# Alternating the second stage's half products with the next pair's gated tiles

## The chip, the cores and the metric

The kernel runs on one core of one Trainium2 chip. The metric is the device time of one execution in microseconds (us). The kernel before took 1480.34 us (median of 3 runs, 1479.32 to 1481.01).

## The reference, cut to what matters

Three blocks follow one another: an attention over 32 memory slots, a gated feed-forward block (512 to 1536 to 512) and a second feed-forward block (512 to 2048 to 512). The change is in the middle block.

```
a = softmax(phi);  k_m = a^T k;  v_m = a^T v            # 8 batches, 8 heads, 576 rows, 32 slots
attn = softmax(q k_m^T / 8);  x = attn v_m              # x: 4608 tokens x 512
g = x @ w_gate;  val = x @ w_val                        # 512 x 1536 each
y = (silu(g) * val) @ w_out                             # 1536 x 512   <- the change is here
h = y @ w_in;  out = elu(h) @ w_out2                    # 512 x 2048, 2048 x 512
```

## The kernel before, in words

All matrix products are made of float32 parts: every operand is split into a high part (`hh`, `hi`) and a low part (`hl`, `lo`), and three matmuls stand for one. The kernel has three stages.

**Stage one** (to about 328 us) does the attention for the 8 batches and the first 4 of the 12 units (128 columns of the hidden dimension) of the gated block, with their share of the output product, which is stored in `p1_d` in DRAM. At its end begins the conversion of weights: a "set" (`sets`, L210) fetches 1 MB of 64-bit weights into a raw tile `wr`, puts float32 numbers into the tile `uq` (`words`, L116, four VectorE instructions; L139 one more), forms eight combinations (`set_split`, L190) and splits them into four tiles `uw`, which the ScalarE queue stores to DRAM (`store_w2`, L171). The `uw` tiles have four buffers.

**Stage two** (about 328 to 770 us) works on the other 8 units, with two batches (a "pair") at a time, so in four groups. In a group, 16 calls of `unit2` (L598) come first. Each makes one gated tile: 12 matmuls for the gate (`pg`), a Silu on ScalarE (`s`, L601), 12 matmuls for the value (`pv`), and one VectorE product into a quarter of a tile `gh` (L603). The weights of these matmuls, `vw`, are made by 16 short matmuls (`vw`, L219) with two ScalarE copies and two VectorE subtractions. PSUM is cut into four tiles of two banks each, called banks 0 to 3 here: 0, 1 and 2 take turns for `pg` and `pv`, and 3 is for `vw`.

Then `down_group` (L627) makes the group's part of the output product by a scheme with seven half-size products (P1 to P7 instead of eight), each of two steps. A step fetches 512 KB of stored weights (`ws`, from `d1_d`, four buffers), splits two pieces of `gh` (L644 on ScalarE, L645 on VectorE) and runs 24 matmuls into the accumulators `acc`. Two sets of accumulator banks, "D" (banks 0 and 1) and "X" (banks 2 and 3), take turns. After a product ScalarE copies the accumulators to `ev` (L613), and GpSimd's queue adds `ev` to `p1_d` with an accumulating DMA (L615), eight of them per group. While the products run, VectorE forms the combinations of `gh` (`COMB`, L649).

Weight sets for stage three run beside all this: `conv[n]` during the units of group n, `late[n]` between the steps of three of its products. What is left over (`rest`) runs in the first slab of **stage three** (from about 770 us), the second feed-forward block.

The order on each engine is decided when the program is built: the code's order, priorities (`tc.high_priority`) and stated successions (`tc.issue_after`) go in, and each engine then runs its own queue strictly in that order. SyncE's queue issues the loads of `ws`, `wr` and the attention result `at2`, ScalarE's queue the stores of `uw`, GpSimd's the accumulating DMAs.

Of the kernel before, what the change touches and what calls it, by code (L numbers as in the profile page):

```python
# [23 lines left out]
T = 512  # L24
# [6 lines left out]
NWO = 4  # L31
# [7 lines left out]
def attention_moe_moe(ctx: ExitStack, tc: tile.TileContext, qT, phiT, kv, kv4, w1g, w1o, w2, out):  # L39
# [13 lines left out]
    wr_p = st_l.enter_context(tc.tile_pool(name="wr", bufs=2))  # L53
# [19 lines left out]
    bk_p = st_bk.enter_context(tc.tile_pool(name="bk", bufs=1, side="right"))  # L73
    wts = [wt_p, st_fr.enter_context(tc.tile_pool(name="wt2", bufs=1))]
# [30 lines left out]

    def fetch_w(src):
        r = wr_p.tile([128, 1024, 2], I32, tag="wr", name="wr")
        fetch_part(r, src, 0, 1)
        return r
# [46 lines left out]
    def load_wo(u2, pool):  # L156
        hi, lo = (pool.tile([128, 2, 512], F32R, tag="w", name=n) for n in ("woh", "wol"))
# [23 lines left out]
    def set_load(kind, q):  # L181
        if (kind, q) not in raw:
            set_fetch(kind, q)
        t = SET[kind, q] = uq_p.tile([128, 8, 256], F32, tag="uq", name="uq")
        load_w(t[:, 2:6].rearrange("p r c -> p (r c)"), raw.pop((kind, q)))
        i = ORDER.index((kind, q)) + 1
        if 1 < i < len(ORDER):
            set_fetch(*ORDER[i])
# [30 lines left out]
    def vw(b, p, pools=(), ps=None):  # L219
        t = VW[b, p] = vx_p.tile([128, 2, 2, 512], F32R, tag="vx", name="vw")  # L220
        ps = ps or [pool.tile([128, 512], F32, tag=tag, name="pvw") for pool, tag in pools]

        def head(j, g):
            r, c = slice(64 * g, 64 * g + 64), slice(32 * j, 32 * j + 32)
            return mm(ps[g][c], lhsT=Bs[b].vt[r, j, :], rhs=WG[p][j][r], start=True, stop=True)  # L225

        together([lambda j=j, g=g: head(j, g) for j in reversed(range(KD)) for g in (1, 0)])
        for g in range(2):
            act(out=t[:, 0, g, :], in_=ps[g], func=AF.Copy)
            if b < NEG and p < UA // 2:  # L230
                mm(ps[g], lhsT=minus, rhs=t[:, 0, g, :], start=False, stop=True, skip_group_check=True)
                act(out=t[:, 1, g, :], in_=ps[g], func=AF.Copy)
                continue
            tt(out=t[:, 1, g, :], in0=ps[g], in1=t[:, 0, g, :].bitcast(F32), op=ALU.subtract)
# [44 lines left out]
    minus = pad_p.tile([128, 128], F32R, tag="minus", name="minus")  # L279
# [178 lines left out]
    raw[0, 0], raw[0, 1] = (wr_p.tile([128, 1024, 2], I32, tag="wr", name="wr") for _ in range(2))  # L458
# [48 lines left out]
    for b in range(B):  # L507
# [10 lines left out]
        if b == B - 2:  # L518
# [8 lines left out]
            fr += sets("first", 0) + [store_w2]  # L527
        if b == B - 1:
            fr += [lambda: load2(0), lambda: load_wg(4, 0, wa_p)]
            fr += [lambda: vw(0, 2, G2)] + sets("first", 1) + [store_w2]  # L530
            fr += [lambda: vw(0, 3, G2), lambda: load_wg(4, 1, wa_p)]
# [34 lines left out]
        if b == B - 3:  # L566
            wts = [wt_p]
            st_fr.close()
            st_ps.close()
# [11 lines left out]
    ev_p = st_r.enter_context(tc.tile_pool(name="ev", bufs=3, side="right"))  # L581
# [8 lines left out]
    turn = [3, 2] + [0, 1, 2] * (2 * NU1 * B)  # L590
# [14 lines left out]
    def vw2(b, p, i):  # L605
        ps = bank2(i, "pvw")
        vw(b, p, ps=[ps[:, 0], ps[:, 1]])


    def add_part(banks, dst):  # L610
        e = ev_p.tile([128, 2, S], F32, tag="e", name="ev")
# [6 lines left out]
    STEPS1 = [("P1", 2, 0, "D", [(0, 0)]), ("P4", 7, 3, "X", [(1, 0)]), ("P6", 1, 0, "D", [(0, 1)]),  # L618
              ("P2", 3, 1, "X", [(0, 0)]), ("P7", 6, 3, "D", [(1, 0), (1, 1)]), ("P5", 0, 2, "X", [(1, 1)]),
              ("P3", 5, 1, "X", [(0, 1)])]  # L620

    COMB = {("P1", 1): (2, 2, 3, 0), ("P1", 3): (2, 2, 3, 1), ("P4", 1): (0, 2, 0, 0), ("P4", 2): (0, 2, 0, 1), ("P6", 2): (3, 3, 0, 0), ("P2", 1): (3, 3, 0, 1),
            ("P7", 1): (1, 1, 0, 0), ("P5", 1): (1, 1, 0, 1)}

    LATE = [("P2", 0), ("P2", 1), ("P7", 0), ("P7", 1), ("P5", 0), ("P5", 1)]

    def down_group(n, g):  # L627
        acc = {}
        store_w2()
        for name, r, k, chain, dst in STEPS1:  # L630
            start = name in ("P1", "P4", "P2", "P5")
            if start:
                acc[chain] = [bank2(i, "acc")[:, :, :HS] for i in ((0, 1) if chain == "D" else (2, 3))]
            if n < B // 2 - 1 and name == "P3":
                for i, (b, p) in enumerate(pairs[8 * n + 8:8 * n + 10]):
                    vw2(b, p, i)
            for j in range(2):
                w = wo_p.tile([128, 2, 2, 256], F32R, tag="w", name="ws")
                last["ws"] = nc.sync.dma_start(out=w.bitcast(F32), in_=d1_d[:, r, 2 * j:2 * j + 2])
                for hf in range(2):  # L640
                    hs = [hs_p.tile([128, 2, HS], F32R, tag=t, name=t) for t in ("hh", "hl")]
                    x = g[k][:, hf, 2 * j:2 * j + 2]
                    with tc.high_priority():
                        act(out=hs[0], in_=x, func=AF.Copy)  # L644
                        last["h"] = last["gate"] = tt(out=hs[1], in0=x, in1=hs[0].bitcast(F32), op=ALU.subtract)  # L645
                    if (name, 2 * j + hf) in COMB:
                        o, a, b, f = COMB[name, 2 * j + hf]
                        with tc.issue_after(last["h"].ins):
                            tt(out=g[o][:, f], in0=g[a][:, f], in1=g[b][:, f],  # L649
                               op=ALU.add if name == "P1" else ALU.subtract)  # L650
                    for i in range(2):
                        for m in range(2):
                            down(acc[chain][m][:, hf], (w[:, i, 0], w[:, i, 1]), (hs[0][:, i], hs[1][:, i]),
                                 slice(128 * m, 128 * m + 128), start and j + i == 0, j + i == 2, not start)
                x = [i for i, p in enumerate(LATE) if p == (name, j)]
                background(late[n], len(late[n]) - len(x))
            add_part(acc[chain], [(2 * n + bi, c) for bi, c in dst])

    def fetch_x():
        xr.append(wr_p.tile([128, KD, T], F32, tag="wr", name="x1l"))  # L660
# [28 lines left out]
    len0 = [len(c) for c in conv]  # L689
    background(conv[0], len0[0] - 2)  # L690
    for n in range(B // 2):
        g = {}
        slot = 0
        for i, (b, p) in enumerate(pairs[8 * n:8 * n + 8]):
            k = i // 2 % 2 * 2 + i // 4
            if i % 2 == 0:
                g[k] = gh_p.tile([128, 2, UA, HS], F32, tag="gh", name="gh")
            for u in (2 * p, 2 * p + 1):
                unit2(b, u, g[k][:, :, u % UA])
                slot += 2  # L700
                background(conv[n], len0[n] * (1 - slot / 24))
            if n == B // 2 - 1:
                if i == 0:
                    fetch_x()
                elif 4 <= i:
                    split_x(i - 4)
            if i < 6:
                vw2(*pairs[8 * n + i + 2], 3)
            if i in (5, 7) and n < B // 2 - 1:
                load2(2 * n + 2 + i // 7)  # L710
        down_group(n, g)
# [6 lines left out]
    wx_p = ctx.enter_context(tc.tile_pool(name="wx", bufs=2, side="right"))  # L718
    op_p = ctx.enter_context(tc.tile_pool(name="op", bufs=3, side="right"))
    g_p = ctx.enter_context(tc.tile_pool(name="g", bufs=2, side="right"))  # L720
# [69 lines left out]
    def x_tasks(t0, ops):  # L790
# [14 lines left out]
        def op(name, src):  # L805
            ops[name] = split2(block(*src), {"A22": wx_p, "S3": wo_p, "S4": wo_p}.get(name, wa_p), ("w", "w"))
# [205 lines left out]
```

## Time and profile before

| | |
|---|---|
| median of 3 runs | 1480.34 us |
| the profiled execution | 1479.91 us, of it 1478.1 us between the first and the last instruction |
| TensorE matmul busy | 1421.1 us (96%) |
| VectorE, ScalarE busy | 1144.5 us (77%), 866.1 us (59%) |
| mean granted TensorE clock | 0.987 of full speed |
| DMA | 341.79 MB, 231 GB/s over the span |

A matmul's row overlaps the next one's, so the pace of TensorE is read from start to start, not from the durations. A wait is read from a row's end: in brackets stand how long the engine was idle before the instruction, and what released it.

### The profile page before, as it was taken

How to read it: one execution, taken by the hardware profiler on the slowest of the kernel's cores; microseconds unless marked ns; L12 is line 12 of the kernel's file. 1: busy time of each engine (PE TensorE's matmuls, PEld its weight loads, DVE VectorE, ACT ScalarE, POOL GpSimd, SP SyncE). 2: the span in 40 equal slices, each digit the busy share in tenths (PEclk: the TensorE clock that was granted, in tenths of full speed). 3: DMA queues.
4: the chain of work that ended last, by engine and by line, in shares of the span. 5: the costliest groups of instructions: out<-in, count | busy, mean ns of one | idle time of the engine just before them, and what ended most of it. 6: DMA issues, size and time to landing. Idle time of an engine off the chain costs nothing.

```text
span 1478.1 us, 23332 instructions
## 1 busy us (share of the span) xinstructions
PE 1421.1 (96%) x9262; PEld 1219.7 (83%) x9262; DVE 1144.5 (77%) x1500; ACT 866.1 (59%) x1300; POOL 48.2 (3%) x75
## 2 busy tenths in 40 slices
PE   5899999999999989979989999999999999999998
PEld 3688788988988988968987888888888888888886
DVE  7998877869778777769876638994889588957884
ACT  4665544545455455445547548755885488548842
POOL 0000000000010010010010000000000000000000
PEclk8999999999999999989999999999999999999999
DMA  9777622664996696695698965766576656676653
GB/s 379 305 275 274 208 98 101 209 243 161 288 323 237 181 321 230 182 316 205 195 310 291 313 199 194 276 212 221 188 247 230 209 192 240 242 227 191 203 208 126
DMA packets 91373, 341.79 MB, mean 231 GB/s; under 512 B 9600, under 2 KB 23936, under 8 KB 72832
## 3 DMA queue, kind: packets, MB, share of 16 engines
q1 hardware_dynamic: 56896, 260.59, 51.0%
q10 hardware_dynamic: 26880, 51.39, 9.2%
q0 software_dynamic: 7488, 28.32, 8.5%
q8 instruction: 73, 1.20, 0.3%
q14 instruction: 36, 0.29, 0.1%
HBM read 251.13 MB, written 89.13 MB: 230 GB/s over the span
## 4 chain that ended last, share of the span: by engine, by line
PE 48%; issue 33%; DMA 9%; DVE 7%; ACT 2%; POOL 1%; ACTq 0%; POOLq 0%; SPq 0%; DVEq 0%
DMA dnd<-uw 4%; PE pv L241 3%; PE acc L246 3%; PE acc L247 3%; PE acc L248 3%; PE pu L738 3%; PE pu L740 3%; PE pu L739 3%; PE pv L242 3%; PE pv L243 3%; PE pg L241 3%; PE pg L243 3%; PE pg L242 3%; PE pvw L225 3%; DMA upd<-uw 2%
## 5 line engine op out<-in xcount | busy, mean ns | idle before, releaser
L740 PE MATMUL pu<-xhi,w 128*128 128x512 f32 x672 | 261.5, 389 | 0.0
L739 PE MATMUL pu<-xlo,w 128*128 128x512 f32 x672 | 261.5, 389 | 0.0
L738 PE MATMUL pu<-xhi,w 128*128 128x512 f32 x672 | 261.4, 389 | 0.0
L767 ACT ACTIVATE xhi<-g 128x1024 fp32r<-128x1024 f32 x120 | 126.6, 1058 | 112.6 <-PE pu L740 70.0
L768 DVE TENSOR_TENSOR xlo<-g,xhi 128x1024 fp32r<-128x1024 f32 x120 | 145.3, 1223 | 48.1 <-ACT xhi L767 48.0
L738 PEld LDWEIGHTS pu<-xhi,w 128*128 128x128 f32 x672 | 126.2, 188 | 26.5
L739 PEld LDWEIGHTS pu<-xlo,w 128*128 128x128 f32 x672 | 126.2, 188 | 26.2
L740 PEld LDWEIGHTS pu<-xhi,w 128*128 128x128 f32 x672 | 126.2, 188 | 25.9
L246 PE MATMUL acc<-hh,ws 128*128 128x288 f32 x448 | 130.8, 296 | 7.8 <-DMA ws<-d1d 7.8
L241 PE MATMUL pv<-at,vw 128*128 128x288 f32 x384 | 119.0, 310 | 17.0 <-ACT s L601 12.7
L247 PE MATMUL acc<-hh,ws 128*128 128x288 f32 x448 | 130.3, 295 | 0.0
L248 PE MATMUL acc<-hl,ws 128*128 128x288 f32 x448 | 123.4, 296 | 0.0
L758 DVE SCALAR_TENSOR_TENSOR et<-et 128x1024 f32<-128x1024 f32 x72 | 88.0, 1222 | 40.7 <-ACT et L757 40.7
L241 PE MATMUL pg<-at,vw 128*128 128x288 f32 x384 | 116.6, 304 | 0.2
L242 PE MATMUL pv<-at,vw 128*128 128x288 f32 x384 | 115.6, 301 | 0.0
L242 PE MATMUL pg<-at,vw 128*128 128x288 f32 x384 | 115.0, 299 | 0.4 <-DVE at L406 0.4
L243 PE MATMUL pv<-at,vw 128*128 128x288 f32 x384 | 115.4, 300 | 0.0
L243 PE MATMUL pg<-at,vw 128*128 128x288 f32 x384 | 114.7, 299 | 0.0
L739 PE MATMUL pd<-xlo,w 128*128 128x512 f32 x288 | 112.0, 389 | 0.0
L738 PE MATMUL pd<-xhi,w 128*128 128x512 f32 x288 | 112.0, 389 | 0.0
L740 PE MATMUL pd<-xhi,w 128*128 128x512 f32 x288 | 112.0, 389 | 0.0
L644 ACT ACTIVATE hh<-gh 128x576 fp32r<-128x576 f32 x112 | 75.8, 683 | 47.7 <-PE acc L247 33.0
(137 smaller groups left out, 3269.1 us busy)
## 6 DMA issues: line engine op xcount, KB each, us to landing
w<-dnd SPq DMA_DIRECT2D x64, 1024.0 KB, 4.9
w<-upd SPq DMA_DIRECT2D x40, 1024.0 KB, 5.7
ws<-d1d SPq DMA_DIRECT2D x56, 512.0 KB, 6.7
w<-upd SPq DMA_DIRECT2D x32, 768.0 KB, 4.6
p1d<-ev POOLq DMA_DIRECT2D x32, 576.0 KB, 10.5
kvr<-kv SPq DMA_DIRECT2D x32, 512.0 KB, 8.3
wr<-w SPq DMA_DIRECT2D x16, 1024.0 KB, 6.1
upd<-uw ACTq DMA_DIRECT2D x32, 512.0 KB, 7.5
```

The source lines that it names most:

```text
L241: mm(ps, lhsT=wh, rhs=ah, start=g == 0, stop=False)
L242: mm(ps, lhsT=wh, rhs=al, start=False, stop=False)
L243: last["pe"] = mm(ps, lhsT=wl, rhs=ah, start=False, stop=g == 1)
L246: mm(ps, lhsT=w[0][:, ms], rhs=hs[0], start=start, stop=False, skip_group_check=skip)
L247: mm(ps, lhsT=w[1][:, ms], rhs=hs[0], start=False, stop=False, skip_group_check=skip)
L248: mm(ps, lhsT=w[0][:, ms], rhs=hs[1], start=False, stop=stop, skip_group_check=skip)
L738: mm(ps, lhsT=w[0], rhs=x[0], start=start, stop=False, skip_group_check=skip)
L739: mm(ps, lhsT=w[0], rhs=x[1], start=False, stop=False, skip_group_check=skip)
L740: last["mm"] = mm(ps, lhsT=w[1], rhs=x[0], start=False, stop=stop, skip_group_check=skip)
L758: stt(out=a, in0=e, scalar=1.0, in1=a, op0=ALU.add, op1=ALU.mult)
L767: last["hi"] = act(out=hi, in_=x, func=AF.Copy)
L768: last["lo"] = tt(out=lo, in0=x, in1=hi.bitcast(F32), op=ALU.subtract)
```

## The change

The groups are no longer "units first, then products". The units of the first pair run alone; then every step of pair n's products is followed by one or two units of pair n+1; only the last pair's products run alone, in the old manner with two sets of banks.

- While products and units alternate, `pg`, `pv` and `vw` share banks 0 and 1, and all seven products use banks 2 and 3 (chain "X"). Their order is P2, P1, P6, P7, P4, P5, P3; P7 goes on from P6 in the same accumulators, so that seven accumulating DMAs are issued in a group instead of eight. The combinations have another table (`MIXCOMB`).
- `gh` has six buffers instead of four, `ws` three instead of four, `ev` two instead of three; in the last group `ev` of P1, P2 and P3 lies in a free `gh` buffer, as does the loaded `x1l`.
- The raw tile `wr` has one buffer after stage one's sixth batch (two before), and the next set is fetched after the current one has been read.
- `vw` in stage two reads both its banks with one ScalarE copy and one VectorE subtraction of 1024 columns, instead of two of 512.
- Sets: none run beside the last group's products. Groups convert 2, 5, 4 and 4 sets, and three sets are left for stage three instead of two.
- In stage three one operand (`S3`) moves to another pool.

```diff
-NWO = 4
+NWO = 3
...
+    wrs = [wr_p, st_fr.enter_context(tc.tile_pool(name="wr2", bufs=1))]
...
-    def sets(kind, q):
-        return [lambda: set_load(kind, q), lambda: set_split(kind, q, (2, 4)),
-                lambda: (store_w2(), set_split(kind, q, (0, 6)))]
+    def sets(kind, q, ahead=True):
+        i = ORDER.index((kind, q)) + 1
+        return [lambda: set_load(kind, q),
+                lambda: (ahead and i < len(ORDER) and set_fetch(*ORDER[i]), set_split(kind, q, (2, 4))),
+                lambda: set_split(kind, q, (0, 6))]
...
+        if both is not None:
+            with tc.high_priority():
+                act(out=t[:, 0], in_=both, func=AF.Copy)
+                tt(out=t[:, 1], in0=both, in1=t[:, 0].bitcast(F32), op=ALU.subtract)
+            return
...
-    gh_p = st_r.enter_context(tc.tile_pool(name="gh", bufs=4, side="right"))
+    gh_p = st_r.enter_context(tc.tile_pool(name="gh", bufs=6, side="right"))
...
-    turn = [3, 2] + [0, 1, 2] * (2 * NU1 * B)
+    MIX = 1000
+    turn = ([3, 2] + [0, 1, 2] * 10 + [0, 1] * MIX)[:32 + MIX]
...
+    MIXED = [("P2", 3, 1, "X", (0, 0)), ("P1", 2, 0, "X", (0, 0)), ("P6", 1, 0, "X", (0, 1)),
+             ("P7", 6, 0, "X", (1, 1)), ("P4", 7, 3, "X", (1, 0)), ("P5", 0, 2, "X", (1, 1)),
+             ("P3", 5, 1, "X", (0, 1))]
...
-    def down_group(n, g):
+    def down_steps(n, g, steps, comb):
         acc = {}
...
+        def step(j, name, r, k, chain, *dst):
+            start = name in ("P1", "P2", "P5", "P4")[:4 if steps is ALONE else 3]
+            if start and j == 0:
                 acc[chain] = [bank2(i, "acc")[:, :, :HS] for i in ((0, 1) if chain == "D" else (2, 3))]
...
+            behind = nullcontext() if steps is ALONE else tc.issue_after(unit_end[-LAG].ins)
...
+            if j == 1:
+                add_part(acc[chain], [(2 * n + b, c) for b, c in dst],
+                         steps is ALONE and name in ("P1", "P2", "P3"))
+
+        return [lambda a=a, j=j: step(j, *a) for a in steps for j in range(2)]
...
-    late = []
-    for n in range(B // 2):
-        late.append([f for _ in range(2 - n // 3) for f in sets(*todo.pop(0))])
-        if n < B // 2 - 1:
-            conv.append([f for _ in range(2 + n // 2) for f in sets(*todo.pop(0))])
+    for n in (5, 4, 4):
+        conv.append([f for _ in range(n) for f in sets(*todo.pop(0))])
...
+            background(fs, n0 * (1 - done[0] / (12 if n == 0 else 16)))
+            if u % 2 == 1:
+                if 8 * n + i + 2 < len(pairs):
+                    vw2(*pairs[8 * n + i + 2])
+                if i in (5, 7) and n < B // 2 - 1:
+                    load2(2 * n + 2 + i // 7)
...
+    for n in range(B // 2 - 1):
+        us = units(n + 1, g[n + 1])
+        for i, f in enumerate(down_steps(n, g[n], MIXED, MIXCOMB)):
+            f()
+            for _ in range(2 if i in (0, 12) else 1):
+                us.pop(0)()
+    fetch_x()
+    for i, f in enumerate(down_steps(B // 2 - 1, g[-1], ALONE, COMB)):
+        f()
+        if 2 <= i < 10 and i % 2 == 0:
+            split_x(i // 2 - 1)
+        store_w2()
```

On TensorE, in the first group of the kernel before, the product P1 ends and P4 begins; `acc_4984` and `acc_4985` are P1's accumulators, `acc_5060` and `acc_5061` those of P4.

```order
L247 MATMUL acc_4985<-hh_5039,ws_5021 128x288
L248 MATMUL acc_4985<-hl_5040,ws_5021 128x288
L246 MATMUL acc_5060<-hh_5064,ws_5062 128x288
L247 MATMUL acc_5060<-hh_5064,ws_5062 128x288
L246 MATMUL acc_5061<-hh_5064,ws_5062 128x288
```

The next product follows in other banks without a matmul between.

On TensorE, after the change, product P2 of the first pair ends (`acc_5001`) and P1 begins in the same bank (`acc_5204`); `pg_5075` and `pv_5053` belong to units of the second pair.

```order
L259 MATMUL acc_5001<-hl_5143,ws_5124 128x288
L252 MATMUL pg_5075<-at2_4855,vw_4917 128x288
L253 MATMUL pg_5075<-at2_4855,vw_4917 128x288
L254 MATMUL pg_5075<-at2_4855,vw_4917 128x288
...
L252 MATMUL pv_5053<-at2_4855,vw_4917 128x288
L253 MATMUL pv_5053<-at2_4855,vw_4917 128x288
L254 MATMUL pv_5053<-at2_4855,vw_4917 128x288
...
L257 MATMUL acc_5204<-hh_5207,ws_5205 128x288
L258 MATMUL acc_5204<-hh_5207,ws_5205 128x288
```

Between the two stand 24 matmuls of units, 12 of `pg_5075` and 12 of `pv_5053`.

On ScalarE, in the first group's products of the kernel before, from the first conversion of one set (`uq`) to the first split of it (`uw_5434`), which needs a buffer that the set before stored from.

```order
L121 ACTIVATE uq_5382<-wr_5254 128x1024
L644 ACTIVATE hh_5555<-gh_4699 128x576
L229 ACTIVATE vw_5504<-pvw_5503 128x512
L613 ACTIVATE ev_5485<-acc_5397 128x576
L644 ACTIVATE hh_5571<-gh_4699 128x576
L613 ACTIVATE ev_5485<-acc_5398 128x576
L601 ACTIVATE s_5605<-pg_5592 128x576
L199 ACTIVATE uw_5434<-uq_5382 128x2x256
```

The same stretch on ScalarE after the change, in the first alternating group.

```order
L126 ACTIVATE uq_5270<-wr_5104 128x1024
L632 ACTIVATE ev_5326<-acc_5203 128x576
L613 ACTIVATE s_5344<-pg_5331 128x576
L662 ACTIVATE hh_5537<-gh_4372 128x576
L662 ACTIVATE hh_5553<-gh_4372 128x576
L613 ACTIVATE s_5415<-pg_5402 128x576
L632 ACTIVATE ev_5492<-acc_5204 128x576
L662 ACTIVATE hh_5620<-gh_4372 128x576
L662 ACTIVATE hh_5636<-gh_4372 128x576
L632 ACTIVATE ev_5492<-acc_5203 128x576
L236 ACTIVATE vw_5443<-pvw_5442 128x1024
L202 ACTIVATE uw_5362<-uq_5270 128x2x256
```

Two Silus, three copies of accumulators and four splits of `gh` now stand between the two, where one Silu, two copies and two splits stood before.

## Rows read from the trace of the kernel before

**Rows 1.** Two groups of stage two: stretch, length, busy PE, PEld, DVE, ACT, POOL; clock, DMA share

```profile
443.00:546.00 103.00, 99.05 (x799) 90.70 (x797) 79.84 (x109) 52.57 (x87) 6.94 (x8) 1.00 0.77 242
546.00:665.00 119.00, 108.41 (x848) 100.22 (x848) 85.82 (x116) 58.33 (x95) 6.93 (x8) 0.95 0.79 247
```

**Rows 2.** TensorE's timeline, the matmuls after a wait: start, us, [idle before, releaser]

```profile
424.63 0.40 PE L246 MATMUL acc<-hh,ws 128*128 128x288 f32 x1 [1.43 <-DMA ws<-d1d]
439.38 0.40 PE L241 MATMUL pv<-at,vw 128*128 128x288 f32 x1 [2.14 <-ACT s L601]
...
535.39 0.40 PE L246 MATMUL acc<-hh,ws 128*128 128x288 f32 x1 [2.31 <-DMA ws<-d1d]
546.68 0.40 PE L241 MATMUL pv<-at,vw 128*128 128x288 f32 x1 [2.05 <-ACT s L601]
653.89 0.61 PE L241 MATMUL pv<-at,vw 128*128 128x288 f32 x1 [3.08 <-ACT ev L613]
665.70 0.61 PE L241 MATMUL pv<-at,vw 128*128 128x288 f32 x1 [7.53 <-ACT s L601]
759.89 0.37 PE L246 MATMUL acc<-hh,ws 128*128 128x288 f32 x1 [1.13 <-DMA ws<-d1d]
764.64 0.40 PE L246 MATMUL acc<-hh,ws 128*128 128x288 f32 x1 [2.92 <-DMA ws<-d1d]
...
795.97 0.50 PE L738 MATMUL pu<-xs,w 128*128 128x512 f32 x1 [3.57 <-DVE g L763]
```

**Rows 3.** Stretches with a lower granted clock (first number after POOL's)

```profile
546.00:550.00 4.00, 3.32 (x18) 3.32 (x19) 2.97 (x5) 3.07 (x6) 0.00 (x0) 0.74 1.02 301
550.00:554.00 4.00, 4.00 (x27) 4.00 (x27) 4.00 (x6) 2.11 (x4) 0.00 (x0) 0.83 1.05 293
654.00:658.00 4.00, 4.00 (x28) 2.98 (x28) 0.36 (x2) 0.38 (x1) 0.86 (x1) 0.61 1.08 298
666.00:670.00 4.00, 4.00 (x18) 4.00 (x18) 3.05 (x5) 2.41 (x4) 0.00 (x0) 0.50 0.64 239
670.00:674.00 4.00, 4.00 (x29) 4.00 (x29) 4.00 (x6) 1.92 (x3) 0.00 (x0) 0.90 0.01 2
796.00:800.00 4.00, 4.00 (x12) 3.17 (x13) 3.96 (x5) 3.97 (x6) 0.00 (x0) 0.64 1.00 402
```

**Rows 4.** ScalarE's waits, 330 to 770 us: waiting line, releaser, us, times, longest

```profile
ACT uw L199 <- DMA dnd<-uw: 13.6, 3, 5.3
ACT uw L199 <- DMA upd<-uw: 10.8, 5, 3.5
```

**Rows 5.** DMA issues, 330 to 770 us: what, queue, count, size, median us to landing

```profile
ws<-d1d SPq DMA_DIRECT2D x55, 512.0 KB, 6.8
...
wr<-w SPq DMA_DIRECT2D x16, 1024.0 KB, 6.1
upd<-uw ACTq DMA_DIRECT2D x32, 512.0 KB, 7.5
dnd<-uw ACTq DMA_DIRECT2D x24, 512.0 KB, 4.5
```

**Rows 6.** TensorE's timeline, 24 matmuls of units and the 16 of a vw

```profile
551.36 0.30 PE L243 MATMUL pg<-at,vw 128*128 128x288 f32 x1
...
554.55 0.29 PE L243 MATMUL pg<-at,vw 128*128 128x288 f32 x1
554.77 1.09 PE L225 MATMUL pvw<-wg,vt 64*32 64x512 f32 x16
```

**Rows 7.** ScalarE by line and shape, 330 to 770 us: count, busy us, mean ns, idle before

```profile
L613 ACT ACTIVATE ev<-acc 128x576 f32<-128x576 f32 x56 | 35.8, 648 | 32.4 <-PE acc L248 31.7 <-DMA at<-atd 0.6
```

**Rows 8.** VectorE in 443 to 546 us by line

```profile
L603 DVE SCALAR_TENSOR_TENSOR gh<-s,pv 128x576 f32<-128x576 f32 x14 | 10.5, 750 | 7.2 <-PE pv L243 7.2
...
L126 DVE SCALAR_TENSOR_TENSOR wc<-wr,wc 128x1024 f32<-128x1024 uint32 x4 | 4.9, 1224 | 0.1
```

**Rows 9.** The same stretch, only what touches `uq`: busy DVE, ACT; clock, DMA

```profile
443.00:546.00 103.00, 28.55 (x41) 12.82 (x19) 1.00 0.77 242
```

More of the change, by code (lines that the diff above doesn't have):

```diff
@@ L220, in vw @@
         t = VW[b, p] = vx_p.tile([128, 2, 2, 512], F32R, tag="vx", name="vw")
-        ps = ps or [pool.tile([128, 512], F32, tag=tag, name="pvw") for pool, tag in pools]
+        both = ps
+        ps = [pool.tile([128, 512], F32, tag=tag, name="pvw") for pool, tag in pools] if both is None else [both[:, g] for g in range(2)]
         def head(j, g):
@@ L457, in attention_moe_moe @@
     z = Bs[0]
-    raw[0, 0], raw[0, 1] = (wr_p.tile([128, 1024, 2], I32, tag="wr", name="wr") for _ in range(2))
+    raw[0, 0], raw[0, 1] = (raw_tile() for _ in range(2))
     fetch_part(raw[0, 0], w1g[0, 0], 0)
@@ L628, in down_group @@
         acc = {}
[L629 to L632, printed above, removed]
+        def step(j, name, r, k, chain, *dst):
+            start = name in ("P1", "P2", "P5", "P4")[:4 if steps is ALONE else 3]
+            if start and j == 0:
                 acc[chain] = [bank2(i, "acc")[:, :, :HS] for i in ((0, 1) if chain == "D" else (2, 3))]
[L634 to L657, printed above, removed]
@@ new lines, in step @@
+            behind = nullcontext() if steps is ALONE else tc.issue_after(unit_end[-LAG].ins)
+            w = wo_p.tile([128, 2, 2, 256], F32R, tag="w", name="ws")
+            last["ws"] = nc.sync.dma_start(out=w.bitcast(F32), in_=d1_d[:, r, 2 * j:2 * j + 2])
+            for hf in range(2):
+                hs = [hs_p.tile([128, 2, HS], F32R, tag=t, name=t) for t in ("hh", "hl")]
+                x = g[k][:, hf, 2 * j:2 * j + 2]
+                with tc.high_priority():
+                    act(out=hs[0], in_=x, func=AF.Copy)
+                    last["h"] = last["gate"] = tt(out=hs[1], in0=x, in1=hs[0].bitcast(F32), op=ALU.subtract)
+                for o, a, b, f in comb.get((name, 2 * j + hf), []):
+                    with tc.issue_after(last["h"].ins):
+                        tt(out=g[o][:, f], in0=g[a][:, f], in1=g[b][:, f], op=ALU.add if (o, a, b) == (2, 2, 3) else ALU.subtract)
+                for i, m in [(i, m) for i in range(2) for m in range(2)]:
+                    with behind if hf + i + m == 0 else nullcontext():
+                        down(acc[chain][m][:, hf], (w[:, i, 0], w[:, i, 1]), (hs[0][:, i], hs[1][:, i]),
+                             slice(128 * m, 128 * m + 128), start and j + i == 0, j + i == 2, not start)
@@ L688, in attention_moe_moe, with units, unit @@
     load2(1)
[L689 to L696, printed above, removed]
-                g[k] = gh_p.tile([128, 2, UA, HS], F32, tag="gh", name="gh")
[L698 to L711, printed above, removed]
+    unit_end = []
+    LAG = 1
+    def units(n, g):
+        fs, n0 = conv[n], len(conv[n])
+        done = [0]
+        def unit(i, k, u):
+            b, p = pairs[8 * n + i]
+            if u % UA == 0:
+                g[k] = gh_p.tile([128, 2, UA, HS], F32, tag="gh", name="gh")
+            unit2(b, u, g[k][:, :, u % UA])
+            unit_end.append(last["pe"])
+            done[0] += 1
+            background(fs, n0 * (1 - done[0] / (12 if n == 0 else 16)))
[4 more added lines that the diff above has]
+                    load2(2 * n + 2 + i // 7)
+        return [lambda i=i, k=i // 2 % 2 * 2 + i // 4, u=2 * pairs[8 * n + i][1] + j: unit(i, k, u)
+                for i in range(8) for j in range(2)]
+    g = [{} for _ in range(B // 2)]
+    background(conv[0], len(conv[0]) - 2)
+    for f in units(0, g[0]):
+        f()
[7 more added lines that the diff above has]
+    for i, f in enumerate(down_steps(B // 2 - 1, g[-1], ALONE, COMB)):
+        f()
+        if 2 <= i < 10 and i % 2 == 0:
+            split_x(i // 2 - 1)
+        store_w2()
     st_r.close()
```

61 lines of the change are left out of this document (35 added, 26 removed).

## The prediction

> **What bounds the kernel now.** I read the page's busy line and slices first: TensorE is busy nearly throughout, so only what TensorE waits for, or does at a lower clock, can be won. Then the stretches of stage two: TensorE has 99.05 us busy in the 103 us of the second group, but 108.41 in the 119 us of the third, at a mean clock of 0.95 [rows 1]. Its pace comes from start to start: from 551.36 to 554.55 us there are 24 matmuls of 288 columns, 0.133 us each, so a unit or a step of a product (24 matmuls) is 3.19 us, and the 16 matmuls of a `vw` take 1.09 us [rows 6]. The sum of matmuls does not change, so this part of the time stays.
>
> Next the waits, in TensorE's timeline [rows 2]. Between 424 and 666 us there are six: two for a `ws` load (1.43, 2.31), three for a Silu (2.14, 2.05, 7.53) and one for an evacuation (3.08), 18.5 us together. They all lie at the end of a group's products or the start of the next units. Why a Silu is late is shown by ScalarE's waits: its splits `uw` wait 24.4 us for their buffers, because the stores `upd<-uw` and `dnd<-uw` have not landed [rows 4], and everything behind them in ScalarE's queue, Silus and evacuations, waits too. The stores take 7.5 and 4.5 us in the median [rows 5], but in these places two sets are converted within six steps (about 19 us), beside 14 loads of `ws` and eight accumulating DMAs.
>
> After a wait TensorE runs slower for a while: a granted clock between 0.50 and 0.90 in five stretches of 4 us [rows 3], that is partly on the lower level of 1.2 GHz. Their losses are 4 x (0.26 + 0.17 + 0.39 + 0.50 + 0.10) = 5.7 us. Stage two thus loses 18.5 + 5.7 = 24.2 us that the order of work causes. Outside this sum stand the last group's end (1.13 + 2.92 us for `ws`) and the first slab of stage three (3.57 us at 796 us and 4 x 0.36 = 1.4 us of clock) [rows 2, 3].
>
> **The change part by part.** *Alternation.* A period of a group keeps 16 units, 14 steps and eight `vw`: (16 + 14) x 3.19 + 8 x 1.09 = 104.4 us. What was bunched is spread. A step now comes about every 7 us (a step and a unit, sometimes a `vw`) instead of every 3.2, and the sets run evenly over 16 units: five sets in 104 us are one per 21 us. A `uw` buffer must be free one set later, and the store leaves one unit (7 us) after the split at the latest, so a store has some 14 us to land, against 7.5 in the median [rows 5]. ScalarE's order shows this distance growing. For `ws`, three buffers give two steps of lead, about 14 us against 6.8 [rows 5]; before, three steps of 3.2 us gave 9.6. So I expect the six waits to go, with their clock stretches. What is late next: a set or a `ws` may still meet a full DMA queue, because the bytes per period hardly change and the share was 0.77 to 0.79 already [rows 1]. I keep one wait of each kind in the three alternating groups, 2.14 + 1.43 = 3.6 us; the bounds are 0 and half of what is there, 12.1 us.
>
> *One set of accumulator banks.* Every product now ends in the banks in which the next begins, 7 in each of three groups, 21 places. Two evacuations of 0.648 us [rows 7] must be done before. The wait of 3.08 us behind an evacuation [rows 2] shows that TensorE does stand still for this. The Trainium skill (PSUM — Partial Sum Buffer, section Terms) says so as a rule: TensorE and a reading engine may not be in one bank at a time. By that rule with nothing between, the 21 places would cost 21 x 1.30 = 27 us. By the order there is a unit between, 24 matmuls, so 3.19 us against 1.30, and ScalarE may be 1.9 us late before it costs anything. I take 0. Bounds: 0 and 27 us.
>
> *Units on two banks.* A `pv` needs the bank that the VectorE product of the unit before (0.750 us, [rows 8]) has read; a step (3.19) and the 12 matmuls of `pg` (1.6) lie between. Slack 4 us: 0.
>
> *VectorE.* The second group of before converts four sets with VectorE busy for 79.84 of 103 us [rows 1]. A set costs 28.55 / 4 [rows 9] plus 1.22 for the line that doesn't touch `uq` [rows 8], 8.4 us. With five sets it would be 88 of 104 us. It stays under TensorE, with little air, in the first alternating group alone. I take 0, at most one set, 8.4 us.
>
> *Joined `vw` copies, seven accumulating DMAs instead of eight.* 30 ScalarE and 30 VectorE instructions fewer and three DMAs fewer, all on engines that TensorE does not wait for here: 0, nor can it add.
>
> *One raw buffer.* At the end of stage one a load must wait until the raw tile has been read. It could bare one landing of 6.1 us [rows 5] in the ScalarE queue; below nothing is excluded, as two buffers were no slower. I take 0, since in ScalarE's order at least a unit's Silu stands between two conversions there.
>
> *The last group alone.* No set is stored beside it any more, which relieves the DMA queues; but three `ws` buffers leave two steps of 3.19 us = 6.4 us for a landing of 6.8 us: 14 x 0.4 = 5.6 us at worst. It can also gain its 4.05 us. I take no change.
>
> *Three sets instead of two in stage three's first slab.* One more set is 8.4 us of VectorE, while the stores of the last group no longer stand before it. Bounds: 5.0 us won, 8.4 lost. I take no change.
>
> **Sum.** The profiled execution took 1479.91 us (span 1478.1 and 1.8 around it), 0.4 below the median of the runs, which I leave out. 1479.9 - 24.2 + 3.6 = 1459.3 us.
>
> **The rivals.**
> - *The DMA lateness moves with the work.* For it: the same bytes, a share near 0.8 already. Against: the second group, with the same four sets, lost less than half of what the third lost. If half of the 24.2 us remains: 1479.9 - 12.1 = 1467.8 us.
> - *Fewer buffers and more sets bite*, in the last group (5.6 us) and as VectorE load (8.4 us): 1459.3 + 14.0 = 1473.3 us. For it: 6.4 us of lead against 6.8; against: both are worst cases of one kind each.
> - *The last group and the slab become clean too*, since no set is converted in the last group: 1459.3 - 4.05 - 5.0 = 1450.2 us. For it: 795.97 waits behind splits that wait for stores. Against: a third set there.
> - *Slower: the single set of accumulator banks.* At each of the 21 places TensorE waits out the evacuation, because ScalarE arrives late from a `uw` that waits for its store (up to 5.3 us, [rows 4]). At 1.30 us each that is 27.3 us, with 5.7 us of lower clock as before: 1479.9 - 24.2 + 33.0 = 1488.7 us. It decides from a mean of 27.2 / 21 = 1.3 us per place on, where the kernel becomes 3 us slower. Against it stands the unit between. The order shows that the alternation is really made, so a change without effect is no case here.
>
> **How the numbers follow.** The forecast has 0.54, half of the lateness staying 0.17, buffers and sets 0.08, the clean end 0.15, the slower one 0.06. The range 1446 to 1472 us reaches from the clean end without the kept 3.6 us (1446.6) to half of the lateness with the last group's 4.05 us lost once more (1471.8); outside lie the slower case, most of the buffers' case and some tails, about 0.15. A change of 0.2% (3 us) is about what a measurement of this kernel can tell from none. Faster by more: all cases but the slower one and their tails, 0.90; within: 0.04; slower: 0.06.
>
> **What would show it right or wrong.** In the profile after, TensorE's rows between the first alternating step and the last group show no wait over 2 us, and a granted clock of 1.00. ScalarE's waits of `uw` for stores fall from 24.4 us to under 10. Stage two ends some 20 us earlier. Wrong would be: `acc` matmuls that wait for `ev` in the alternating groups (the banks), `pv` that waits for `gh` (VectorE), or waits for `ws` in the last group above 4 us (three buffers).

## The result, and the profile after

The changed kernel takes 1461.26 us (median of 4 runs, 1458.51 to 1463.84), the kernel before beside it 1480.67 us (1479.32 to 1482.88). The ratio is 0.9867 with the 95% interval [0.9844, 0.9891], a gain of 1.3%. The forecast was 1459.3 us. The profiled execution, the shortest of the four, took 1458.51 us (span 1456.7, mean granted clock 0.993, before 0.987). That is 21.4 us below the profiled execution before, and this pair is what the following account explains.

The page's busy line of the changed kernel: busy us, share of the span, instructions.

```profile
PE 1417.2 (97%) x9262; PEld 1215.0 (83%) x9262; DVE 1140.3 (78%) x1470; ACT 864.2 (59%) x1270; POOL 45.5 (3%) x72
```

Where the alternation runs, stretches of 100 us of the changed kernel (columns as in [rows 1]: busy PE, PEld, DVE, ACT, POOL; then clock, DMA share and GB/s):

```profile
400.00:500.00 100.00, 98.97 (x792) 91.50 (x791) 86.57 (x114) 58.71 (x89) 6.21 (x7) 1.00 0.93 287
500.00:600.00 100.00, 99.88 (x810) 92.05 (x809) 80.08 (x105) 54.51 (x82) 6.05 (x7) 1.00 0.83 244
600.00:700.00 100.00, 100.00 (x807) 93.56 (x792) 79.67 (x105) 56.10 (x87) 6.06 (x7) 1.00 0.84 249
```

TensorE is busy for 99 to 100 us of each 100, at a clock of 1.00. The mean DMA share has gone up, from 0.77 to 0.79 [rows 1] to 0.83 to 0.93, with nothing lost by it there. But the mean before hides two levels. The first row below is a block of products in the kernel before, the second the units that follow it:

```profile
489.00:540.00 51.00, 48.69 (x382) 46.74 (x381) 46.27 (x59) 29.03 (x47) 5.34 (x7) 1.00 0.95 270
540.00:601.00 61.00, 58.95 (x476) 52.86 (x475) 39.74 (x59) 29.41 (x47) 1.60 (x2) 0.97 0.61 219
```

Beside products the DMA engines were full (0.95 to 0.99 in the three blocks), beside units they were not (0.61 to 0.64). After the change, stretches of 20 us from 400 to 700 us have 0.74 to 0.98: the peaks are spread into the gaps.

TensorE's timeline of the changed kernel: the matmuls from 380 to 700 us that wait for a `ws`, then the last group and the first matmul of stage three (columns as in [rows 2]):

```profile
385.93 0.40 PE L257 MATMUL acc<-hh,ws 128*128 128x288 f32 x1 [0.36 <-DMA ws<-d1d]
480.47 0.37 PE L257 MATMUL acc<-hh,ws 128*128 128x288 f32 x1 [0.91 <-DMA ws<-d1d]
...
710.80 0.37 PE L257 MATMUL acc<-hh,ws 128*128 128x288 f32 x1 [1.06 <-DMA ws<-d1d]
737.81 0.37 PE L257 MATMUL acc<-hh,ws 128*128 128x288 f32 x1 [1.00 <-DMA ws<-d1d]
741.58 0.40 PE L257 MATMUL acc<-hh,ws 128*128 128x288 f32 x1 [0.34 <-ACT ev L632]
747.91 0.48 PE L257 MATMUL acc<-hh,ws 128*128 128x288 f32 x1 [4.47 <-DMA ws<-d1d]
...
754.82 0.50 PE L772 MATMUL pu<-xs,w 128*128 128x512 f32 x1 [0.35 <-ACT ev L632]
```

The same first matmul of stage three in the kernel before:

```profile
770.36 0.47 PE L738 MATMUL pu<-xs,w 128*128 128x512 f32 x1 [0.68 <-DMA w<-upd]
```

Stage three begins 15.5 us earlier (770.36 to 754.82). What follows it takes 1456.7 - 754.8 = 701.9 us instead of 1478.1 - 770.4 = 707.7, 5.8 us less; 15.5 + 5.8 are the 21.4 to within rounding.

- The six waits of [rows 2], 18.5 us, are now 0.36 + 0.91 = 1.3 us. The clock loss of 5.7 us in the alternating groups [rows 3] is gone.
- The last group got worse. Its waits for `ws` were 1.13 + 2.92 us and are now 1.06 + 1.00 + 4.47, with 0.34 for an evacuation. After the longest the clock drops, which before did not happen there (row below): 4 x 0.43 = 1.7 us. Together 4.5 us more.
- The start of stage two (310 to 380 us) has 4.0 us of waits, seven of 0.17 to 0.72 us, against two with 1.6 us before: 2.4 us more.
- The first slab of stage three: the wait for `g` of 3.57 us and the clock loss of 1.4 us behind it are gone.

The sum is -(18.5 - 1.3) - 5.7 + 4.5 + 2.4 - 5.0 = -21.0 us, against 21.4 measured.

The stretch of the changed kernel behind its longest wait:

```profile
748.00:752.00 4.00, 4.00 (x19) 4.00 (x20) 1.12 (x2) 0.00 (x0) 0.87 (x1) 0.57 1.01 426
```

ScalarE's waits for DMAs in the changed kernel, 330 to 750 us, all there are:

```profile
ACT uq L126 <- DMA wr<-w1o: 5.2, 1, 5.2
...
ACT wg L126 <- DMA wr<-w1g: 2.6, 1, 2.6
```

No `uw` waits for a store any more; before they waited 24.4 us [rows 4]. DMA issues of the changed kernel in the stretch of [rows 5], last number the median us to landing:

```profile
ws<-d1d SPq DMA_DIRECT2D x55, 512.0 KB, 5.0
...
upd<-uw ACTq DMA_DIRECT2D x32, 512.0 KB, 6.5
...
dnd<-uw ACTq DMA_DIRECT2D x24, 512.0 KB, 7.1
```

As medians over the whole stage the stores hardly look faster: `upd` lands in 6.5 us instead of 7.5, but `dnd` in 7.1 instead of 4.5. These medians mix the two levels above. In the kernel before, the `upd` issued in the block of products from 489 to 540 us and in the units from 540 to 601 us, and the `dnd` issued in the block from 601 to 649 us:

```profile
upd<-uw ACTq DMA_DIRECT2D x4, 512.0 KB, 14.8
upd<-uw ACTq DMA_DIRECT2D x12, 512.0 KB, 3.5
dnd<-uw ACTq DMA_DIRECT2D x4, 512.0 KB, 19.8
```

In the changed kernel, `upd` from 500 to 600 us and `dnd` from 600 to 700 us:

```profile
upd<-uw ACTq DMA_DIRECT2D x12, 512.0 KB, 6.5
dnd<-uw ACTq DMA_DIRECT2D x14, 512.0 KB, 6.2
```

So the stores that were late, those beside products, do land sooner; the others land later, and nobody waits for them. The loads of `ws` land sooner too, 5.0 instead of 6.8 us.

### The profile page after: what moved, and what is told of

It is laid out like the page before. It is cut to its first block, busy times and chain, and to the rows that moved or that the text cites. A ratio compares the mean times of both kernels' runs of the same rounds, so it can differ in the third digit from the quotient of the medians.

```text
span 1456.7 us, 23256 instructions
## 1 busy us (share of the span) xinstructions
PE 1417.2 (97%) x9262; PEld 1215.0 (83%) x9262; DVE 1140.3 (78%) x1470; ACT 864.2 (59%) x1270; POOL 45.5 (3%) x72
## 2 busy tenths in 40 slices
DMA packets 90940, 340.01 MB, mean 233 GB/s; under 512 B 9552, under 2 KB 23888, under 8 KB 72400
## 4 chain that ended last, share of the span: by engine, by line
PE 50%; issue 35%; DVE 6%; DMA 6%; ACT 1%; POOL 1%; POOLq 0%; SPq 0%; DVEq 0%; ACTq 0%
PE acc L257 4%; PE acc L259 4%; PE acc L258 4%; PE pu L772 3%; PE pu L774 3%; PE pu L773 3%; PE pvw L231 3%; PE pv L252 3%; DMA ws<-d1d 3%; PE pg L252 3%; PE pv L254 3%; PE pv L253 3%; PE pg L253 3%; PE pg L254 3%; PE pd L257 2%
## 5 line engine op out<-in xcount | busy, mean ns | idle before, releaser
L257 PE MATMUL acc<-hh,ws 128*128 128x288 f32 x448 | 133.3, 299 | 8.2 <-DMA ws<-d1d 7.8
L258 PE MATMUL acc<-hh,ws 128*128 128x288 f32 x448 | 132.8, 297 | 0.0
L259 PE MATMUL acc<-hl,ws 128*128 128x288 f32 x448 | 130.9, 298 | 0.0
L252 PE MATMUL pv<-at,vw 128*128 128x288 f32 x384 | 116.4, 303 | 2.3 <-ACT s L613 1.3
L253 PE MATMUL pv<-at,vw 128*128 128x288 f32 x384 | 113.9, 297 | 0.0
L254 PE MATMUL pv<-at,vw 128*128 128x288 f32 x384 | 113.7, 296 | 0.0
```

The lines of the kernel that those rows point to most:

```text
L252: mm(ps, lhsT=wh, rhs=ah, start=g == 0, stop=False)
L253: mm(ps, lhsT=wh, rhs=al, start=False, stop=False)
L254: last["pe"] = mm(ps, lhsT=wl, rhs=ah, start=False, stop=g == 1)
L257: mm(ps, lhsT=w[0][:, ms], rhs=hs[0], start=start, stop=False, skip_group_check=skip)
L258: mm(ps, lhsT=w[1][:, ms], rhs=hs[0], start=False, stop=False, skip_group_check=skip)
L259: mm(ps, lhsT=w[0][:, ms], rhs=hs[1], start=False, stop=stop, skip_group_check=skip)
```

## The experiments

The prediction named two causes for the late stores in one breath: two sets within six steps, and the products in one block with their `ws` loads and accumulating DMAs. The first question was which of them it is: the *bunched sets* or the *bunched products*. Every kernel was timed beside the kernel before.

**The change again,** without an edit, as the control in the same series, on the same chip, as the old order with its sets spread, the bunched sets and the `ws` in more buffers.

> The changed kernel itself, run beside the others so that they share its chip. Both theories expect what was measured: 1458.5 to 1463.8 us. No wait of TensorE over 1 us in the alternating groups, and 5 to 7 us of waits for ws loads in the last group.

Measured: 1461.02 us (1460.19 to 1462.02), ratio 0.9849 [0.9834, 0.9864]. The alternating groups lose 1.6 us for `ws`; the last group 7.4 us for `ws` and 0.34 for an evacuation. The pattern is reproduced, the last group's weakness included. Its stage three begins at 758.35 us.

**The old order with its sets spread** over units and steps: only half of what the change does.

```diff
+    for n in range(1, B // 2):
+        conv[n] += late[n]
...
-                background(conv[n], len0[n] * (1 - slot / 24))
+                background(conv[n], len0[n] * (1 - (slot / 24 if n == 0 else slot * 1.84 / 104)))
...
+                    background(conv[n], len0[n] * (1 - (59 + 3.2 * k1) / 104))
```

> The kernel before with its order of units first, products then, but with the weight sets of each group spread evenly over its units and the steps of its products (before: two sets within six steps). Theory A (bunching: the stores of two sets in 19 us fill the DMA queues, the split tiles come free late, ScalarE stands still): most of the 24.2 us of stage two goes without any alternation, ScalarE's waits of uw for stores fall from 24.4 us to under 10, time 1460 to 1468 us. Theory B (cover: a late ScalarE costs nothing only where units and products alternate): the accumulating DMAs and ws loads of the products still fill the queues, TensorE still waits 12 us or more at the ends of the groups, time 1472 us or more.

Measured: 1472.49 us (1471.34 to 1473.17), ratio 0.9925 [0.991, 0.994]; the second row below is the end of its stage two, in TensorE's timeline, the third its first slab:

```profile
733.00 0.58 PE L246 MATMUL acc<-hh,ws 128*128 128x288 f32 x1 [2.37 <-DMA ws<-d1d]
...
757.30 0.50 PE L743 MATMUL pu<-xs,w 128*128 128x512 f32 x1 [0.34 <-ACT ev L613]
...
788.06 0.79 PE L743 MATMUL pu<-xs,w 128*128 128x512 f32 x1 [6.73 <-DVE g L768]
```

ScalarE of the same kernel in front of that slab:

```profile
777.01 0.63 ACT L199 ACTIVATE uw<-uq 128x512 fp32r<-128x512 f32 x1 [5.18 <-DMA dnd<-uw]
...
782.86 0.63 ACT L199 ACTIVATE uw<-uq 128x512 fp32r<-128x512 f32 x1 [5.22 <-DMA dnd<-uw]
```

Neither theory got this one whole. Spreading the sets alone takes away ScalarE's waits for stores and, with them, the long waits for a Silu in stage two. Its stores beside products still land in 10.2 to 11.5 us at a DMA share of 0.99 to 1.03, but each buffer is needed later. Four waits for `ws` stand between 330 and 700 us, 7.8 us together where there were 3.7, as bunched products would have it. Stage three begins at 757.30 us, as early as in the control (758.35). What is lost against the change is lost behind that: the stores of the last sets now fall on the first slab, where `uw` waits 5.2 us twice and TensorE 6.73 us for `g`.

**The change with its sets bunched** again, into the first half of each period: the other half.

```diff
-            background(fs, n0 * (1 - done[0] / (12 if n == 0 else 16)))
+            background(fs, n0 * (1 - done[0] / (12 if n == 0 else 8)))
```

> The changed kernel with the sets of each alternating group squeezed into its first eight units (five, four and four sets in about 52 us instead of 104). Theory A (bunching) expects ScalarE's waits for stores to return, 15 us or more, and TensorE waits of 10 us or more in the alternating groups: 1470 to 1480 us. Theory B (cover) expects ScalarE to wait, but TensorE to lose under 4 us: 1459 to 1466 us.

Measured: 1464.46 us (1459.82 to 1469.16), ratio 0.9872 [0.9845, 0.9899], which overlaps with the control's interval; its runs spread over 9 us, and the profile is of one of 1462.32. ScalarE's only waits for a DMA from 380 to 705 us, and then TensorE's main ones from 380 to 700 us:

```profile
ACT uq L126 <- DMA wr<-w: 5.1, 3, 2.3
```

```profile
PE pv L252 <- DVE vw L237: 1.6, 2, 1.3
PE pvw L231 <- ACT s L613: 1.0, 2, 0.7
PE pg L252 <- ACT s L613: 0.7, 1, 0.7
```

No wait for a store came back in this execution, and TensorE waits 3.5 us instead of the control's 1.6. With the products spread, the sets may be bunched: the theory that bunched sets are enough by themselves falls. The bunching is a little weaker than before, one set in 10 to 13 us instead of two in 19, so a tighter one is not excluded.

**The old order without accumulating DMAs** in the first three groups; their sums are not added into the result.

```diff
-            add_part(acc[chain], [(2 * n + bi, c) for bi, c in dst])
+            add_part(acc[chain], [(2 * n + bi, c) for bi, c in dst] if n == 3 else [])
```

> The kernel before without the accumulating DMAs of the first three groups (24 of 32; that part of the sum is left out of the output), everything else in its place, the sets bunched as before. Theory A' (the stores of uw are late because eight accumulating DMAs and 14 ws loads crowd the queues in the 45 us of a group's products): ScalarE's waits of uw for stores fall from 24.4 us to under 8, TensorE's waits between 420 and 670 us from 18.5 us to under 6, time 1458 to 1466 us. Rival A (two sets within 19 us are too much for four buffers by themselves): ScalarE still waits 12 us or more, TensorE 10 us or more, time 1470 us or more.

Measured: 1454.67 us (1452.52 to 1456.0), ratio 0.9828 [0.9811, 0.9844]. ScalarE's only wait for a store from 330 to 770 us, and then its DMA issues from 400 to 700 us:

```profile
ACT uw L199 <- DMA dnd<-uw: 4.5, 1, 4.5
```

```profile
ws<-d1d SPq DMA_DIRECT2D x37, 512.0 KB, 4.1
upd<-uw ACTq DMA_DIRECT2D x32, 512.0 KB, 4.1
...
dnd<-uw ACTq DMA_DIRECT2D x20, 512.0 KB, 3.7
```

With sets and products where they were, the store waits fall from 24.4 to 4.5 us, `ws` lands in 4.1 us, and TensorE has no wait from 337 to 734 us. In the same stretch `ws` took 8.5 us before. In the blocks of products the DMA share is 0.70 to 0.72 instead of 0.95 to 0.99, and the stores issued there land in 5.0 to 5.1 us. So the third ingredient, 24 accumulating DMAs within the blocks of products, is needed to make the stores and the `ws` loads late; whether by their number of bytes or by their price per byte, this run alone doesn't tell, and no run took away as many bytes of another kind. The change leaves 21 of them in, and gets most of the same by spacing them out.

**The last group with one set of banks** for its sums, as the alternating groups have it, but with no unit between two products: the slower rival's case laid bare.

```diff
-    ALONE = [("P1", 2, 0, "D", (0, 0)), ("P4", 7, 3, "X", (1, 0)), ("P6", 1, 0, "D", (0, 1)), ("P2", 3, 1, "X", (0, 0)),
...
+    ALONE = list(MIXED)
...
-    for i, f in enumerate(down_steps(B // 2 - 1, g[-1], ALONE, COMB)):
+    for i, f in enumerate(down_steps(B // 2 - 1, g[-1], ALONE, MIXCOMB)):
```

> The changed kernel with the last group's products, which have no units beside them, on the one set of accumulator banks as well (seven products in the order of the alternating groups). It shows what a place costs where no unit covers the evacuation. Theory (the cover of 24 matmuls is why one set costs nothing): TensorE now waits for ScalarE's ev at about six places, 1 to 2 us each, 6 to 12 us together in the last group, and the kernel is 5 to 12 us slower than the changed one, 1466 to 1473 us. Rival (the scheduler and the two halves of a product hide the evacuation in any case): under 0.4 us per place, time within 3 us of the changed kernel.

Measured: 1464.67 us (1462.71 to 1469.02), ratio 0.9901 [0.9878, 0.9923]. TensorE's waits for evacuations from 700 to 810 us, and then ScalarE's wait that stands behind the longest:

```profile
PE acc L257 <- ACT ev L632: 6.3, 6, 4.6
```

```profile
ACT ev L632 <- DMA p1d<-ev: 4.7, 1, 4.7
```

One of the other five, on TensorE, and ScalarE's two copies before it:

```profile
727.61 0.40 PE L257 MATMUL acc<-hh,ws 128*128 128x288 f32 x1 [0.35 <-ACT ev L632]
```

```profile
726.90 1.19 ACT L632 ACTIVATE ev<-acc 128x576 f32<-128x576 f32 x2 [1.92 <-PE acc L259]
```

Five of the six waits are 0.34 to 0.35 us, far below the 1.30 us of two full evacuations. The copies begin at 726.90 us, before the old product's last matmul at 726.97, and end at 728.09. The new product starts at 727.61 on its first half of banks, while the second copy still runs; its fourth matmul, by the program's order the first into the second half, starts at 728.15. The sixth, 4.59 us, is another thing: the evacuation's target was still being read by an accumulating DMA. By an estimate from these waits, 21 uncovered places at 0.35 us cost 7.4 us, not 27.

The time is above the control's (ratio 0.9849 [0.9834, 0.9864]), but the profiled execution, the shortest of the four, doesn't show why: its stage three begins at 757.17 us, the control's at 758.35, because the last group's waits for `ws` are 1.3 us here instead of 7.4.

**The last group's `ws` in more buffers,** the four that stage three loads its weights into later, from the fourth step on.

```diff
-            w = wo_p.tile([128, 2, 2, 256], F32R, tag="w", name="ws")
+            at = 2 * [s[0] for s in steps].index(name) + j
+            w = (vx_p.tile([128, 2, 2, 256], F32R, tag="vx", name="ws") if steps is ALONE and at > 2 else
+                 wo_p.tile([128, 2, 2, 256], F32R, tag="w", name="ws"))
```

> The changed kernel; from the fourth step of the last group on, the ws loads land in the four buffers of vw instead of the three of ws, which gives one more step of lead and also keeps stage three's first four loads of 1 MB behind these buffers. Theory (the last group's wait of 4.47 us and the 1.7 us of lower clock after it come from these 4 MB overtaking the last ws load): the wait falls under 1.5 us and the kernel gains 4 to 6 us, 1454 to 1457 us. Rival (the accumulating DMAs and the ws loads alone fill the queues): the waits stay at 5 us or more, time as the changed kernel; or the first weights of stage three now come late and TensorE waits for them instead.

Measured: 1453.72 us (1452.84 to 1455.23), ratio 0.9797 [0.9781, 0.9814], below the control's interval on the same chip. TensorE's waits from 690 to 810 us:

```profile
PE pu L774 <- DVE g L799: 3.7, 2, 2.9
PE pu L774 <- DMA w<-upd: 0.7, 1, 0.7
PE acc L257 <- ACT s L613: 0.5, 1, 0.5
PE acc L257 <- ACT ev L632: 0.3, 1, 0.3
```

The waits for `ws` are gone. The edit does two things at once, and the run doesn't part them. The last `ws` load goes out one step earlier against the first load of stage three (733.09 and 736.27 us; 736.85 and 737.21 in the changed kernel). And stage three's first loads of 1 MB, which want the same four buffers, come one by one (736.27, 739.46, 744.31, 746.43 us) instead of four within 4 us. That `ws` load lands in 5.8 us instead of 11.0. In place of the waits for `ws` the first slab waits for `g` again, and VectorE's timeline of the same kernel says for what:

```profile
765.78 1.28 DVE L799 TENSOR_TENSOR g<-et,pu 128x512 f32<-128x512 f32 x2 [3.10 <-DMA p1d<-ev]
```

The first tile of `g` lies in memory where an evacuated sum still waits for its accumulating DMA.

**The evacuated sum of P3 elsewhere**, in one of `ev`'s own buffers, first with the edit before, then also with sets of 5, 5 and 4 in the three alternating groups instead of 5, 4 and 4.

```diff
-                         steps is ALONE and name in ("P1", "P2", "P3"))
+                         steps is ALONE and name in ("P1", "P2"))
...
-    for n in (5, 4, 4):
+    for n in (5, 5, 4):
```

> The kernel with the last group's ws in the vw buffers (1453.7 us), and P3's evacuation in the last group in an ev buffer instead of a free gh buffer. Theory (the first slab's wait of 2.85 us is for memory: the first g tile lies where P3's evacuated sum waits for its accumulating DMA): the wait goes, 2 to 4 us faster with the clock it keeps, 1449 to 1452 us. Rival (the wait is the late wr load, the DMA queues are full): no change, 1453 to 1455 us.

Measured: 1455.95 us (1454.76 to 1457.81), ratio 0.9835 [0.9816, 0.9853]. TensorE now waits 2.5 us for `ev` and 2.0 for `g`, since `ev` waits 7.4 us for the DMA of an earlier sum. The wait moved, no more.

> As the one before, with five sets in the second alternating group too, so that two sets instead of three are left for the first slab of stage three. Theory (VectorE has air for a fifth set, as in the first alternating group): no new waits in the alternating groups, less DMA in the slab, the same or up to 3 us faster, 1447 to 1452 us. Rival (VectorE at 88 of 104 us is too tight): waits of TensorE for VectorE over 2 us in the second alternating group, slower.

Measured: 1452.63 us (1452.09 to 1455.35), ratio 0.9819 [0.9802, 0.9836]. VectorE carries the 14th set without a wait of TensorE's; the first slab still has 2.3 us for `ev`. It can't be told from the run with more `ws` buffers alone.

**The start of stage two.** There ScalarE waits 5.2 us for a raw load (above). Three kernels: the one with the `ws` buffers again; the same with the raw weights of two sets fetched ahead into `gh` buffers that are still free; and that with 5, 5 and 4 sets.

```diff
+    for q in (2, 3):
+        raw["first", q] = gh_p.tile([128, 2, UA, HS], F32, tag="gh", name="wrg")...
...
+    for q in (2, 3):
+        fetch_part(raw["first", q], w1o[UA // 2 + q], 0, 1)
```

> The kernel with the last group's ws in the vw buffers once more, as the measure for the two beside it: 0.980 of the kernel before, as measured.

Measured: 1456.36 us (1453.67 to 1458.19), ratio 0.9842 [0.9826, 0.9859].

> As e8; the raw weights of the two sets that the first group converts are fetched at the start of stage two into two gh buffers that are free then, so they don't queue for the one raw buffer. Theory (the waits of 0.4 to 0.9 us at the start of stage two, some 3 us together, come from the single raw buffer: ScalarE stands 3 to 5 us before a conversion whose load had to wait): ScalarE's wait for that load goes, TensorE's waits between 320 and 380 us fall from about 3 us to under 1.5, 1 to 3 us faster than e8. Rival (these waits come from VectorE's queue, whatever the load): no change.

Measured: 1453.53 us (1452.36 to 1458.3), ratio 0.9832 [0.9813, 0.9851]. ScalarE's wait for that load from 310 to 380 us, in the kernel without the edit and then with it:

```profile
ACT uq L126 <- DMA wr<-w1o: 3.8, 1, 3.8
```

```profile
ACT uq L126 <- DMA wrg<-w1o: 0.7, 1, 0.7
```

3.1 us of ScalarE's wait go, but TensorE's waits there only fall from 2.6 to 1.9 us, and the times overlap. The late raw load is real and is a small part of what TensorE waits for; the rest are single waits of 0.3 to 0.6 us for ScalarE, VectorE and once a `ws` load.

> As e9, with five sets in the second alternating group and two left for stage three's first slab. Theory (less DMA and VectorE work in the slab, air for a fifth set beside the alternation): the first slab's wait of 2.85 us shrinks, 0 to 3 us faster than e9. Rival: the slab's wait is for memory that an accumulating DMA still reads, no change.

Measured: 1455.2 us (1450.71 to 1455.94), ratio 0.983 [0.9811, 0.9848]. No gain: the first slab waits 4.8 us for `g`.

On the one chip where both ran, the kernel with more `ws` buffers in the last group gains 7.3 us over the change (1453.72 against 1461.02 us; ratios 0.9797 and 0.9849, intervals apart). Its repetition took 1456.36 us, without the change beside it, and its interval [0.9826, 0.9859] overlaps with both of the change's own ([0.9844, 0.9891] and [0.9834, 0.9864]). So the gain is shown in one series and not confirmed in the other, and among this kernel and the ones built on it none is shown to be the best.

## Why the prediction was right, point by point

- **The six waits and the clock.** Right, and right in the trace: no wait above 0.91 us in the alternating groups, a clock of 1.00, no wait of `uw` for a store. The 3.6 us that were kept were too many by 2.3.
- **Why stores were late.** Right in that the lateness went, incomplete in the reason. The prediction set a distance of 14 us between split and next use against a landing of 7.5 us, and read the DMA share as 0.77 to 0.79; both are means over two levels. Beside products the share was 0.95 to 0.99 and the stores took 14.8 to 19.8 us in the median, which 14 us of distance would not have covered. Two things can cure that. The old order with its sets spread shows the distance at work: the share in the blocks stays at 1, the stores still take 10.2 to 11.5 us, and ScalarE doesn't wait. The change, the bunched sets and the run without accumulations show the other: the load on the DMA engines is levelled or lowered, and the stores land sooner (6.2 to 8.1 us from 400 to 700 us in the change, 4.7 to 8.7 by half periods with the sets bunched, 5.0 to 5.1 in the blocks without accumulations). And the prediction let the sets carry the cause. The runs say: accumulating DMAs inside a block of products; spreading either the sets or the products is enough for the stores, and the `ws` loads want the products spread or the accumulations gone.
- **One set of accumulator banks.** Taken at 0, measured 0 in the alternating groups. The upper bound of 27 us, and with it the slower rival at 1488.7 us, was mis-sized: an uncovered place costs 0.35 us where the buffers are free, because reading the first half of the banks begins before the product has ended.
- **VectorE, the joined copies, units on two banks.** Taken at 0. VectorE is busy for 86.57 of 100 us in the first alternating group (88 of 104 were worked out, a little less), and no `pv` waits for it between 380 and 700 us.
- **The last group alone.** Mis-sized: 0 taken, 4.5 us lost (2.8 of waits, 1.7 of clock), within the bounds given. This is the larger part of why stage two ends 15.5 us earlier and not some 20. The landing of 6.8 us was a median of all of stage two. In the last group three loads came late, and the last of them cost 4.47 of the 6.5 us. SyncE's issues of the changed kernel around it (start, us), and then the DMA issues from 735 to 737.1 us with the median us to landing:

```profile
736.85 0.32 SPq L657 DMA_DIRECT2D ws<-d1d  x1
...
737.21 3.96 SPq L761 DMA_DIRECT2D w<-upd  x4
```

```profile
p1d<-ev POOLq DMA_DIRECT2D x2, 576.0 KB, 9.6
ws<-d1d SPq DMA_DIRECT2D x1, 512.0 KB, 11.0
```

  The load is issued at 736.85, lands 11.0 us later at 747.85, and TensorE goes on at 747.91. Behind it in the same queue come stage three's first four loads of 1 MB, beside it two accumulating DMAs. That these lengthen it is argued from the order. The kernel with more `ws` buffers cures it, by more lead and by loads of 1 MB that come later, and it is open which of the two does it. The prediction's own sign of failure, `ws` waits above 4 us in the last group, came true.
- **One raw buffer.** Taken at 0. It bares one landing in ScalarE's queue, as bounded (5.2 us against 6.1), of which TensorE pays a fraction. The start's 2.4 us are otherwise not settled: they are seven single waits of 0.17 to 0.72 us, four for ScalarE and three for VectorE.
- **Three sets in the first slab.** Taken at 0, measured 5.0 us won, the better end of the bounds. Before, `uw` waited 4.90 and 1.83 us for `dnd` stores in the slab; after, it waits for none. The old order with its sets spread shows the same the other way round: its four stores issued from 750 to 754 us, just before the slab, take 28.3 us to land in the median, and the slab loses 6.73 us.
- **The clean-end rival** was half right: the slab became clean, the last group did not. The misses (-2.3 for the kept waits, +4.5, +2.4, -5.0) nearly cancel, so the profiled execution came out 0.8 us from the sum (1458.5 against 1459.3), and the median 2.0 us from it, with four terms wrong by more than 2 us each. That the number is so close is luck; that the waits of the alternating groups and their clock loss would go, 22.9 of the 24.2 us, is not.

## What to carry to other kernels

When an engine waits for buffers whose stores are late, look at what else fills the DMA engines in the same microseconds, and at accumulating transfers first; spacing them between other work can free the stores at nearly the same bytes (340.01 MB here instead of 341.79). A landing time or a DMA share taken over a whole stage says little where the stage has two levels, or on its edges, where the next stage's large loads are issued behind it: read both in the stretch where the lead is used. A bound for a wait on an accumulator should come from a place where the wait stands uncovered, not from the sum of the reads.

## What the hardware showed

An accumulating DMA is dear for its bytes, by the time that its packets took. The queues of the kernel before, 443 to 546 us (packets, MB, share of the 16 engines): q0 holds the accumulating transfers, q1 the loads.

```profile
q1 hardware_dynamic: 2716, 13.30, 36.9%
q0 software_dynamic: 978, 3.99, 21.2%
```

The same of the changed kernel, 704 to 755 us:

```profile
q0 software_dynamic: 1029, 4.23, 48.4%
q1 hardware_dynamic: 2029, 9.04, 47.0%
```

Per MB an accumulating transfer takes 0.212 x 103 x 16 / 3.99 = 88 us of one engine in the first stretch and 0.484 x 51 x 16 / 4.23 = 93 in the second; a load 46 and 42. It is twice the price in both, and seven of them in the last 51 us of stage two take as much of the engines as all the loads.

The other is the price of a reused accumulator: 0.34 to 0.35 us at five places, about half of one evacuation of 0.648 us [rows 7].
